# First batch's attention in 32x64 score tiles, turned in quarters, its values taken in halves, in two groups of blocks a pair

## The chip, the cores and the metric

The kernel runs on one core of a Trainium2 chip. The metric is device microseconds (us) of one execution, the median of several runs. Engines are called as the profile calls them: PE (TensorE matmul), PEld (its weight loads), DVE (VectorE), ACT (ScalarE), POOL (GpSimd), SP (the queue that issues most DMAs).

## The reference, cut to what matters

Windowed attention of 4 batches, 8 heads, 576 positions of 64, then two feed-forward layers over the 2304 tokens. Heads 0 to 3 see the last 32 positions, heads 4 to 7 see every fourth of the last 128.

```python
scores = scale * np.matmul(q, k.transpose(0, 1, 3, 2))
mask_plain = (rel >= 0) & (rel < window)                                   # window = 32
mask_dil = (rel >= 0) & (rel < window * dilation) & (rel % dilation == 0)  # dilation = 4
scores = scores - np.max(scores, axis=-1, keepdims=True)
attn = np.exp(scores); attn = attn / (np.sum(attn, axis=-1, keepdims=True) + 1e-09)
attn_out = np.matmul(attn, v)
x = g1(x @ w_in) @ w_out       # g1(h) = h - tanh(h)
x = g2(x @ w_in2) @ w_out2     # g2(h) = h / (1 + exp(-h))
```

The weights arrive in 64 bits and are turned on the chip into two f32 parts each ("high" and "low" words, then a leading and a trailing part).

## The kernel before, in words

The work on one batch's attention goes by pairs of heads, 4 pairs a batch: pairs 0 and 1 are plain, pairs 2 and 3 dilated (their positions are sorted by residue, so that a window of 32 neighbours remains). A pair's 576 queries are 9 blocks of 64 (`NB`, `QB`). In every tile the two heads of a pair stand above each other: rows 0 to 63 and rows 64 to 127.

For the first batch each pair goes through 3 units of 3 blocks (`UB`, `NU`). Of one unit: a matmul writes the mask into a PSUM bank (L401), six matmuls add 64x96 scores to it (64 queries of one head, 96 keys, L416), DVE takes the maxima (L451), ACT the exponentials, one instruction a block, with the sum on the side (L469), DVE the inverse sums (L474, L475), DVE or POOL scales (L479, `normed`), PE transposes three blocks of 96 keys (L501), ACT copies them to `pT` (L146), PE multiplies by the values (L510), ACT and DVE split the result into two parts of `X` (`x_hi`, `x_lo`, L553). Ahead of it PE transposes q and k (L363, L372), which ACT and DVE copy to qT and kT. An f32 matmul stands twice in the trace, since it is done in two passes, and an f32 transpose once.

From the second batch on a pair is done in two groups of 5 and 4 blocks (`GROUPS`), with 32x64 score tiles (L408): 32 queries of one head against 64 keys, four tiles of a block in four strips of 32 columns of the array. DVE transposes there what PE transposes in the first batch.

All this is mixed with the first feed-forward layer of block 0 (512 tokens, 16 slices `f` of the hidden width): per slice 12 matmuls into `h` and 12 into `y` (L578; four groups of three each), the gate (ACT L1146, DVE L1147), its two parts `gg` (ACT L146, DVE or POOL L1149), and the preparation of a piece of each weight matrix: three ACT operations (L180, L185, L146), DVE L190, POOL L194, and DVE or POOL L203.

The order of all engines up to the end of block 0's slices is set by a list of operations (`op(...)`) with the engines that may do each and a planned length, its predecessors and a rank; `play` walks through the list and gives each engine the operation that could begin first, by these planned lengths. Where it finds PE without work it puts in small matmuls on the identity (`idle`, L108). The engines then execute their streams in that order, each waiting for what it needs. SP's and POOL's DMA issues are in the list too. What follows block 0's slices is in a fixed order.

## Time and profile before

| | |
|---|---|
| median of 3 runs | 842.42 us (841.42 to 842.45) |
| the profiled execution | 843.15 us, of which 841.4 us from the first to the last instruction (the span) |
| PE busy | 828.4 us, 98% of the span |
| DVE, ACT, POOL busy | 68%, 50%, 24% |
| mean granted TensorE clock | 0.999 |

A row of the timeline gives the start, the length, engine, line, operation, what is written and read, and how many instructions are merged in the row; in brackets the idle time of the engine before it and what ended it. The distance between the starts of two neighbouring rows of a busy engine is what the first of them costs.

### The profile page before, as it was taken

The page shows a single profiled execution, that of the slowest core. Times are in us where ns is not written, and L with a number is a line of the kernel's source. Part 1 is how long each engine was busy: PE and PEld are TensorE (multiplying, and loading weights), DVE is VectorE, ACT ScalarE, POOL GpSimd, SP SyncE. Part 2 cuts the span into 40 slices and gives each one's busy share as a digit, 9 for nine tenths or more (in the row PEclk, how much of TensorE's full clock was granted, in tenths as well). Part 3 has the DMA queues.
Part 4 walks back from the last instruction along what each step waited for, and adds up shares of the span by engine and source line. Part 5 has one row for each costly group of instructions (what it writes and reads, how often), then busy time and mean ns, then how long its engine had stood idle before and what let it go on. Part 6 is the DMA issues. An engine that isn't in the chain of part 4 may idle for free.

```text
span 841.4 us, 16392 instructions
## 1 busy us (share of the span) xinstructions
PE 828.4 (98%) x6102; PEld 735.1 (87%) x6102; DVE 568.5 (68%) x1010; ACT 424.2 (50%) x960; POOL 198.9 (24%) x236
## 2 busy tenths in 40 slices
PE   8989999999999999999999999999999999999998
PEld 5767788888887888888899999888999999999997
DVE  3788987566676664566664677548766897567764
ACT  5898985355555443665553343445332454233442
POOL 8555442043333231111100000000025100054000
PEclk9999999999999999999999999999999999999999
DMA  9987353655569414477769199749897676998542
GB/s 219 296 219 196 83 141 91 179 124 120 125 142 260 101 43 147 152 268 267 281 240 374 50 366 360 265 150 365 298 409 265 245 287 253 341 353 290 184 169 57
DMA packets 168319, 184.58 MB, mean 219 GB/s; under 512 B 88848, under 2 KB 130864, under 8 KB 167216
## 3 DMA queue, kind: packets, MB, share of 16 engines
q1 hardware_dynamic: 167408, 182.69, 67.2%
q8 instruction: 48, 0.79, 0.4%
q0 software_dynamic: 832, 0.85, 0.4%
q14 instruction: 31, 0.25, 0.1%
HBM read 137.89 MB, written 45.61 MB: 218 GB/s over the span
## 4 chain that ended last, share of the span: by engine, by line
PE 92%; ACT 3%; DVE 2%; SPq 1%; issue 1%; DMA 0%; POOL 0%; ACTq 0%; DVEq 0%; POOLq 0%
PE y L578 43%; PE h L578 27%; PE q L578 16%; PE h L510 1%; SPq L301 1%; PE y L416 1%; PE s L408 1%; PE s L510 1%; PE y L974 1%; PE h L363 1%; PE y L501 1%; DVE pT L492 1%; PE o L510 1%; ACT st L180 1%; ACT st L185 0%
## 5 line engine op out<-in xcount | busy, mean ns | idle before, releaser
L578 PE MATMUL y<-gg,w 128*128 128x512 f32 (+1 forms) x960 | 218.3, 370 | 2.6 <-DVE gg L1149 2.6
L578 PE MATMUL h<-x,w 128*128 128x512 f32 (+1 forms) x960 | 218.4, 370 | 0.7 <-POOL w L203 0.7
L578 PEld LDWEIGHTS y<-gg,w 128*128 128x128 f32 x960 | 167.2, 189 | 34.4 <-DVE gg L1149 3.8
L578 PEld LDWEIGHTS h<-x,w 128*128 128x128 f32 x960 | 167.3, 189 | 31.8 <-POOL w L203 1.1
L578 PE MATMUL y<-wr,gs 128*128 128x256 f32 (+1 forms) x840 | 123.5, 298 | 0.0
L578 PEld LDWEIGHTS y<-wr,gs 128*128 128x128 f32 x840 | 112.6, 191 | 4.6
L726 ACT ACTIVATE G<-tmp 128x384 f32<-128x384 f32 (+1 forms) x48 | 32.9, 686 | 117.1 <-DVE tmp L717 117.1
L749 DVE TENSOR_TENSOR gs<-G,gs 128x768 fp32r<-128x768 f32 x64 | 62.7, 985 | 42.3 <-ACT gs L748 42.1
L748 ACT ACTIVATE gs<-G 128x768 fp32r<-128x768 f32 x64 | 53.5, 844 | 70.0 <-PE y L578 44.4
L578 PE MATMUL q<-x,wr 128*128 128x384 f32 x432 | 82.8, 335 | 0.0
L605 DVE TENSOR_TENSOR g<-h,g 128x512 f32<-128x512 f32 (+1 forms) x64 | 39.8, 622 | 59.3 <-ACT g L604 59.1
L578 PEld LDWEIGHTS q<-x,wr 128*128 128x128 f32 x432 | 75.5, 188 | 0.5 <-DVE tmp L717 0.5
L1463 ACT ACTIVATE gg<-g 128x512 fp32r<-128x512 f32 (+1 forms) x64 | 37.1, 579 | 74.7 <-DVE g L605 73.6
L604 ACT ACTIVATE g<-h 128x512 f32<-128x512 f32 (+1 forms) x64 | 34.7, 542 | 67.7 <-PE h L578 65.2
L1465 DVE TENSOR_TENSOR gg<-g,gg 128x512 fp32r<-128x512 f32 (+1 forms) x64 | 40.3, 630 | 41.7 <-ACT gg L1463 39.6
L727 DVE SCALAR_TENSOR_TENSOR G<-G,tmp 128x384 f32<-128x384 f32 (+1 forms) x48 | 41.3, 861 | 34.3 <-ACT G L726 34.3
L194 POOL TENSOR_TENSOR st<-st 128x512 int32<-128x512 int32 x36 | 39.6, 1109 | 78.3 <-DVE st L190 43.2
L578 PE MATMUL y<-x,wr 128*128 128x384 f32 x288 | 57.7, 334 | 0.0
L578 PE MATMUL h<-x,wr 128*128 128x384 f32 x288 | 57.7, 334 | 0.0
L578 PE MATMUL q<-wr,gs 128*128 128x256 f32 (+1 forms) x348 | 57.6, 301 | 0.0
L578 PEld LDWEIGHTS q<-wr,gs 128*128 128x128 f32 x348 | 49.3, 191 | 2.4
L578 PEld LDWEIGHTS y<-x,wr 128*128 128x128 f32 x288 | 50.6, 188 | 0.2 <-DVE x L638 0.2
(161 smaller groups left out, 1142.3 us busy)
## 6 DMA issues: line engine op xcount, KB each, us to landing
wr<-w_in SPq DMA_DIRECT2D x72, 512.0 KB
wr<-w_out SPq DMA_DIRECT2D x66, 512.0 KB
st<-in_moe_w_in_dram SPq DMA_DIRECT2D x32, 256.0 KB
st<-in_moe_w_out_dram SPq DMA_DIRECT2D x16, 512.0 KB
st_in<-in_moe_w_in_dram SPq DMA_DIRECT2D x32, 256.0 KB
w_in<-mixed SPq DMA_DIRECT2D x8, 1024.0 KB
wr<-w_in SPq DMA_DIRECT2D x24, 256.0 KB
x<-y_hi SPq DMA_DIRECT2D x6, 768.0 KB
```

The costliest lines, as they stand in the source:

```text
L180: engine.activation(out=high, in_=high, func=AF.Prelu, scale=2.0 ** -112, alpha=2.0 ** 32)
L194: engine.tensor_tensor(out=high, in0=high, in1=self.low.bitcast(I32), op=ALU.add)
L510: nc.tensor.matmul(o[64 * j:64 * j + 64, n - n0, :], self.v[j][:, n, :], pT[:, n, j, :], start=True, stop=True)
L578: nc.tensor.matmul(o, stat[a], mov[b], start=first and n == 0, stop=last and n == 2, skip_group_check=more)
L604: nc.scalar.activation(out=g, in_=h, func=AF.Tanh)
L605: nc.vector.tensor_tensor(out=g, in0=h, in1=g, op=ALU.subtract)
L726: nc.scalar.activation(out=g, in_=h, func=AF.Tanh, scale=0.5)
L727: return lambda: nc.vector.scalar_tensor_tensor(out=g, in0=g, scalar=1.0, in1=h, op0=ALU.add, op1=ALU.mult)
L748: nc.scalar.activation(out=gs[:, 0], in_=g, func=AF.Copy)
L749: nc.vector.tensor_tensor(out=gs[:, 1], in0=g, in1=gs[:, 0].bitcast(F32), op=ALU.subtract)
L1463: nc.scalar.activation(out=gg[:, 0], in_=g, func=AF.Copy)
L1465: nc.vector.tensor_tensor(out=gg[:, 1], in0=g, in1=gg[:, 0].bitcast(F32), op=ALU.subtract)
```

## The change

For the first batch alone:

- Two groups of blocks a pair (5 and 4) in place of three units of 3. The mask `mask` (96 keys wide) is gone; `near` (64 wide), which the later batches use, is built directly, by POOL on 32 rows and by three DVE copies, in place of an ACT copy and four later copies.
- Scores in 32x64 tiles, added to a mask of 64 columns.
- The four of the eight groups that `WHOLE` names take a shift on DVE (`shifted`), one ACT instruction for all exponentials of the group (`exps_whole`) and the sums on DVE (`totals`); the other four do one ACT instruction a block as before, over 64 columns.
- The probabilities are turned by ordinary matmuls against a reordered identity (`turn`), 128 rows by 32 columns each, four side by side in quarters of the array, and land as `turned`: 32 queries of both heads, 128 keys. ACT or DVE copies them.
- The values are taken in 64x64 quarters of the array, 32 columns each (`halves`), into two fixed banks, one for each half of a block's queries.
- v needs 32 more rows, a second copy of keys: one more load a head for pairs 0 and 1 (SP), a copy of 32 rows for pairs 2 and 3 (`double_v`). The values of pair 2 are loaded by SP, behind the first two weight pieces, in place of POOL.
- `pT` is zeroed later. Ranks and planned lengths of the list change.

```diff
     NM = NB + GROUPS[0][1]
-    mask = cpool.tile([P, NM, KB], BF16, name="mask")
-    nc.gpsimd.memset(mask[0:QB], 0.0)
...
-    nc.scalar.copy(out=mask[QB:], in_=half)
+    near = cpool.tile([P, NM, NARROW], BF16, name="near")
+
+    def build_near():
+        band = near[0:32, NM - 1]
+        nc.gpsimd.memset(band, 0.0)
+        keep(band, [[-1, NARROW]], 32, 1)
+        keep(band, [[1, NARROW]], -1, -1)
+        nc.vector.tensor_copy(out=near[0:32, :NM - 1], in_=band.unsqueeze(1).to_broadcast([32, NM - 1, NARROW]))
+        nc.vector.tensor_copy(out=near[32:QB], in_=band.unsqueeze(1).to_broadcast([32, NM, NARROW]))
+        for n in range(NB + 1):
+            for i in range(2):
+                for start in range(0, S, CLS) if n < NB else (0,):
+                    at = start - (QB * (n % NB) + 32 * i - 32)
+                    if 0 < at < NARROW:
+                        keep(near[0:32 * (i + 1), n, 0:at], [[0, at]], at - 33 + 32 * i, -1)
+        nc.vector.tensor_copy(out=near[QB:], in_=near[0:QB])
...
+                if self.first:
+                    out.append(lambda e, j=j, src=src: e.dma_start(
+                        out=self.v[j][KB:], in_=bass.AP(src.tensor, src.offset, [[D, P - KB], [QB * D, NB], [1, D]])))
             return out
+
+        def double_v(self, engine):
+            copy(engine, self.vt[KB:], self.vt[32:64])
...
             for n in range(n0, n1):
...
-                for j in range(2):
-                    nc.tensor.matmul(
-                        s[QB * j:QB * (j + 1), m, at:],
-                        self.qT[64 * j:64 * j + 64, QB * n:QB * n + QB],
-                        keys[64 * j:64 * j + 64],
-                        start=False, stop=n == n1 - 1,
-                    )
+                for i in range(2):
+                    q0 = QB * n + 32 * i
+
+                    at = HALO if masked and q0 == 0 else 0
+                    keys = self.kT[:, q0 - HALO + at:q0 + 32] if masked else kT1[:, q0:q0 + NARROW]
+                    for j in range(2):
+                        r = slice(64 * j, 64 * j + 64)
+                        nc.tensor.matmul(s[QB * j + 32 * i:QB * j + 32 * i + 32, n - n0, at:], self.qT[r, q0:q0 + 32], keys[r],
+                                         start=not masked, stop=not masked or n == n1 - 1)
...
+        def shifted(self, n0, n1):
+            nb = self.nb.pop(n0)
+            nc.vector.tensor_tensor(out=self.p[:, n0:n1], in0=self.ps.pop(n0), in1=nb.unsqueeze(2).to_broadcast([P, n1 - n0, NARROW]), op=ALU.add)
+
+        def exps_whole(self, n0, n1):
+            pr = self.p[:, n0:n1]
+            nc.scalar.activation(out=pr, in_=pr, func=AF.Exp)
+
+        def totals(self, n0, n1):
+            nc.vector.tensor_reduce(out=self.total[:, n0:n1], in_=self.p[:, n0:n1], axis=AX.X, op=ALU.add)
...
-            for m in range(UB):
-                nc.tensor.transpose(t[:, m, :], self.p[:, UB * u + m, :], one[F32])
...
+        def turn(self, n0, n1, bank):
+            t = bank[:, :(n1 - n0) * QB].rearrange("p (n j q) -> p n j q", j=2, q=32)
+            unit = one[F32].rearrange("p (j i q) -> p i j q", j=2, i=2)
+            self.pt[n0] = t
+            for n in range(n0, n1):
+                for g in range(4):
+                    i, kk = divmod(g, 2)
+                    kk ^= i
+                    nc.tensor.matmul(t[32 * g:32 * g + 32, n - n0], self.p[:, n, 32 * kk:32 * kk + 32], unit[:, i], start=True, stop=True)
...
+        def halves(self, n0, n1, at):
...
+            for n in range(n0, n1):
+                for i in range(2):
+                    r = slice(64 * i, 64 * i + 64)
+                    for j in range(2):
+                        nc.tensor.matmul(o[i][64 * j:64 * j + 64, n - n0], self.v[j][r, n], pt[r, n, j], start=True, stop=True)
...
-    SLOT0, SLOT, UNIT0, UNIT = 46.0, 5.2, 12.0, 1.8
+    SLOT0, SLOT, UNIT0, UNIT = 36.0, 5.2, 12.0, 4.5
...
-    NEXT0, NEXT = 60.0, 16.0
+    NEXT0, NEXT = 50.0, 16.0
+    WHOLE = (1, 0, 1, 0, 1, 0, 1, 0)
...
-            v_on = {"P": 0.62} if p.dil else {"S": 0.55}
...
+            on_p = p.c == NPAIR - 1
+            got[p, "v"] = [op({"P": 0.95} if on_p else {"S": 0.5}, fn, rank=p.c + (1.15 if p.dil else 0.2),
+                              late=0.25 if p.dil else 0.5, lag=3.0 if on_p else 0.0) for fn in p.v_loads()]
+            if p.dil:
+                got[p, "v"].append(op({"P": 1.5, "V": 0.8, "A": 1.1}, p.double_v, got[p, "v"], UNIT0 + UNIT * p.c, port=True))
```

Three places of the order. First PE, from the k transposes of pair 1 (`kin`) on. `one` and `late` are identities, `prob` the probabilities, `s` and `o` the banks of the values, `y_...` the banks of the scores and of the transposes. Before:

```order
L372 MATMUL h<-late,kin 64x96 x6
L401 LDWEIGHTS one
L401 MATMUL y_338<-mask,one 128x288
L416 MATMUL y_338<-kT,qT 64x96 x6
L501 MATMUL y_354<-late,prob 96x128 x3
L401 LDWEIGHTS one
L401 MATMUL y_359<-mask,one 128x288
L416 MATMUL y_359<-kT,qT 64x64 x2
L416 MATMUL y_359<-kT,qT 64x96 x4
L510 MATMUL o<-pT,v 64x64 x6
```

Of the change, after ten filler matmuls on `one` behind those k transposes:

```order
L410 MATMUL y_385<-near,one 128x320
L419 MATMUL y_385<-kT,qT 32x32 x2
L419 MATMUL y_385<-kT,qT 32x64 x18
L515 MATMUL y_415<-late,prob 32x64 x20
L515 MATMUL y_438<-late,prob 32x64 x16
L528 MATMUL s<-turned,v 64x32 x2
L528 MATMUL o<-turned,v 64x32 x2
```

Scores of pair 1 now come ahead of both turns and all values of pair 0, and one step holds 20 or 16 small matmuls where it held 6 or 3.

Second ACT, from the last scaled pieces of the attention to the first gate (`g<-h`): `st_...` are weight pieces, `w` their leading parts. Before, from the last turned copy on:

```order
L146 ACTIVATE pT<-y_804 96x384
L146 ACTIVATE w<-st_190 128x512
L185 ACTIVATE st_192<-st_192 128x512
L146 ACTIVATE x<-s 128x192
L180 ACTIVATE st_191<-st_191 128x512
L185 ACTIVATE st_191<-st_191 128x512
L180 ACTIVATE st_194<-st_194 128x512
L146 ACTIVATE w<-st_192 128x512
L185 ACTIVATE st_194<-st_194 128x512
L1146 ACTIVATE g<-h 128x512
```

Of the change, from the last turned copy that ACT does:

```order
L146 ACTIVATE turned<-y_954 128x320
L185 ACTIVATE st_198<-st_198 128x512
L180 ACTIVATE st_201<-st_201 128x512
L146 ACTIVATE w<-st_199 128x512
L146 ACTIVATE x<-s 128x5x32
L146 ACTIVATE x<-o 128x5x32
L146 ACTIVATE x<-s 128x4x32
L146 ACTIVATE x<-o 128x4x32
L146 ACTIVATE w<-st_198 128x512
L185 ACTIVATE st_201<-st_201 128x512
L180 ACTIVATE st_200<-st_200 128x512
L1190 ACTIVATE g<-h 128x512
```

When the attention's last `x` is written, ACT has issued 8 operations on weight pieces before the change and 12 with it.

Third PE again, where the second batch's first scores (32x64 tiles into `s` and `o`) stand among the feed-forward matmuls. Before:

```order
L578 MATMUL h<-x,w 128x512 x12
L408 MATMUL s<-kT,qT 32x64 x20
L408 MATMUL o<-kT,qT 32x64 x16
L578 MATMUL h<-x,w 128x512 x3
L578 MATMUL y_918<-gg,w 128x512 x3
```

Of the change:

```order
L607 MATMUL y_1118<-gg,w 128x512 x3
L607 MATMUL h<-x,w 128x512 x3
L607 MATMUL y_1119<-gg,w 128x512 x3
L607 MATMUL h<-x,w 128x512 x3
L607 MATMUL y_1120<-gg,w 128x512 x3
L419 MATMUL s<-kT,qT 32x64 x20
L419 MATMUL o<-kT,qT 32x64 x16
L607 MATMUL y_1121<-gg,w 128x512 x3
```

These scores stood behind 7 groups of three feed-forward matmuls and now stand behind 23; those of the next pair behind 17 and now behind 49.

## Rows read from the trace of the kernel before

**Rows 1.** The page: span, and PE's line (busy us, share, instructions).

```profile
span 841.4 us, 16392 instructions
PE 828.4 (98%) x6102; PEld 735.1 (87%) x6102; DVE 568.5 (68%) x1010; ACT 424.2 (50%) x960; POOL 198.9 (24%) x236
```

**Rows 2.** Busy time in four stretches (start:end, length, then each engine's us).

```profile
core 0: us, PE busy (x) PEld busy (x) DVE busy (x) ACT busy (x) POOL busy (x), PEclk, DMA share, GB/s
6.60:43.70 37.10, 34.85 (x580) 26.21 (x578) 22.99 (x71) 30.26 (x111) 24.27 (x50) 1.00 1.03 268
43.70:96.30 52.60, 48.14 (x435) 37.71 (x434) 44.62 (x85) 48.11 (x119) 28.45 (x27) 1.00 0.66 171
96.30:200.00 103.70, 103.70 (x775) 85.01 (x774) 73.17 (x141) 63.59 (x167) 32.01 (x40) 1.00 0.49 126
200.00:841.00 641.00, 636.65 (x4306) 584.35 (x4304) 427.14 (x714) 280.98 (x566) 108.16 (x107) 1.00 0.69 236
```

**Rows 3.** Timeline of PE: one unit's steps and a pair's k transposes.

```profile
28.05 0.30 PE L401 MATMUL y<-mask,one 128*128 128x288 bf16 x1
28.27 0.71 PE L416 MATMUL y<-kT,qT 64*64 64x96 f32 x12
28.92 0.57 PE L510 MATMUL o<-pT,v 96*64 96x64 f32 x12
29.42 0.53 PE L501 MATMUL y<-late,prob 128*96 128x128 f32 x3
29.88 1.22 PE L363 MATMUL h<-late,kin 72*64 72x72 f32 x32
```

**Rows 4.** Timeline of PE: the second batch's first scores.

```profile
47.63 0.76 PE L408 MATMUL s<-kT,qT 64*32 64x64 f32 x40
48.21 0.63 PE L408 MATMUL o<-kT,qT 64*32 64x64 f32 x32
48.77 0.96 PE L578 MATMUL h<-x,w 128*128 128x512 f32 x3
```

**Rows 5.** Timeline of PE: the rows with idle time ahead, 6.6 to 100 us.

```profile
11.19 0.72 PE L372 MATMUL h<-late,qin 96*64 96x96 f32 x12 [1.04 <-ACT kT L146]
...
39.04 0.53 PE L501 MATMUL y<-late,prob 128*96 128x128 f32 x3 [1.09 <-POOL prob L479]
...
45.13 2.57 PE L578 MATMUL h<-x,w 128*128 128x512 f32 x10 [0.66 <-POOL w L203]
...
50.29 1.65 PE L578 MATMUL y<-gg,w 128*128 128x512 f32 x6 [0.56 <-DVE gg L1149]
...
58.13 0.76 PE L408 MATMUL s<-kT,qT 64*32 64x64 f32 x40 [1.24 <-DVE kT L393]
...
72.15 0.96 PE L578 MATMUL y<-gg,w 128*128 128x512 f32 x3 [1.70 <-DVE gg L1149]
...
95.98 0.98 PE L578 MATMUL y<-gg,w 128*128 128x512 f32 x3 [0.30 <-DVE gg L1149]
```

**Rows 6.** Timeline of ACT around the mask copy.

```profile
9.12 1.31 ACT L250 COPY mask<-mask 64x1344 bf16<-64x1344 bf16 x1
10.46 1.18 ACT L146 ACTIVATE kT<-h 128x288 f32<-128x288 f32 x2
```

**Rows 7.** Chain that ended last: six records of ACT's exponentials (three blocks).

```profile
36.81 0.96 ACT prob L469 x6
```

**Rows 8.** Groups by line and shape, 0 to 100 us (busy us, mean ns).

```profile
L146 ACT ACTIVATE pT<-y 96x384 f32<-96x384 f32 x12 | 5.8, 486 | 2.4 <-PE y L501 2.1
L451 DVE TENSOR_REDUCE sum<-prob 128x5 f32<-128x320 f32 x3 | 1.4, 476 | 0.0
```

**Rows 9.** Chain that ended last, ahead of the wait at 72.15.

```profile
67.08 2.21 DMA kin<-in_k_dram
69.41 0.13 DVE kT L393
...
71.40 0.70 DVE gg L1149
```

**Rows 10.** Timeline of PE: the attention's last values.

```profile
43.16 0.57 PE L510 MATMUL s<-pT,v 96*64 96x64 f32 x12
43.74 0.73 PE L578 MATMUL h<-x,w 128*128 128x512 f32 x2
```

More of the change, by code (lines that the diff above doesn't have):

```diff
@@ L255, in tile_kernel @@
     qT1 = cpool.tile([P, S], F32, name="qT")
-    near = cpool.tile([P, NM, NARROW], BF16, name="near")
     pT = cpool.tile([KB, NB, 2, QB], F32, name="pT")
-    nc.gpsimd.memset(pT, 0.0)
+    turned = [cpool.tile([P, NB, 2, 32], F32, name="turned")]
     class Pair:
@@ L514, in values @@
             if self.dil:
-                parts = [(a, b, src[:, a - s0:b - s0]) for a, b in self.cut(s0, s1)]
+                out = [(self.columns(a, b), src[:, a - s0:b - s0]) for a, b in self.cut(s0, s1)]
             else:
@@ new lines, in tile_kernel @@
+            ring_t.leave(b)
+            a = op({"T": 0.15 + 0.115 * m}, lambda e, p=p, g=g, i=i: p.halves(*g, 160 * (i % 3)), [b, *got[p, "v"], *ring_o.take()], r)
+            if n1 == NB:
+                ring_v.leave(a)
+            ends = []
+            for z in range(2):
+                b = op({"A": 0.32}, lambda e, p=p, n0=n0, z=z: p.x_hi(e, (n0, z)), [a], r)
+                ends.append(op({"V": 0.32}, lambda e, p=p, n0=n0, z=z: p.x_lo((n0, z)), [b], r))
+            ring_o.leave(*ends)
@@ L1038, in tile_kernel @@
+            x_done.setdefault(p.c, []).extend(ends)
+            if n1 == NB:
                 at_v = 4 * p.c + 2
@@ L1076, in tile_kernel @@
                 in_room[NF - len(MORE_IN) + place - 1 - len(MORE_OUT)] = (c,)
-        left = {"bank": tuple(x_done[NPAIR - 1][-2:]), "pT": tuple(ring_v.take() + ring_v.take() + ring_v.take()),
+        left = {"bank": tuple(x_done[NPAIR - 1]), "pT": (),
                 "q": (), "k": (), "v": (first[2].last,)}
         normed = {}
-        def narrow(e, g):
-            copy(e, near[32 * g:32 * g + 32], mask[32 * g:32 * g + 32, :, 32 * (g % 2):32 * (g % 2) + NARROW])
-        narrows = [op({"V": 0.35, "P": 0.9}, lambda e, g=g: narrow(e, g), x_done[0][:1], NEXT0 - 30, port=True) for g in range(4)]
+        zero = op({"P": 1.05}, lambda e: e.memset(pT, 0.0), x_done[0][:1], NEXT0 - 10)
+        left["pT"] = (zero,)
         def front(p):
```

140 lines of the change are left out of this document (64 added, 76 removed).

## Prediction

> **What bounds the kernel now.** I read the page first: PE is busy in 828.4 of 841.4 us [rows 1]. A share over the whole span hides where PE waits, so next come four stretches [rows 2]. From 96.3 to 200 us PE is busy in all of the 103.7 us, and after that in 636.65 of 641. What the change can win there is only what arrives from ahead of it: the order behind is fixed and its loads are set off by PE's own progress, so I take it that each us won before 96 is a us won at the end. Ahead of it lie two stretches of different kinds. Up to 43.7 us, the attention of the first batch, PE is busy 34.85 of 37.1 us and ACT 30.26. From 43.7 to 96.3, block 0's feed-forward, PE is busy 48.14 of 52.6 us, but ACT also 48.11 and DVE 44.62: there the feeding of PE is nearly as full as PE. The timeline of PE then gives the waits [rows 5]: seven, 6.59 us in all, two in the attention (1.04 and 1.09) and five behind it (0.66, 0.56, 1.24, 1.70, 0.30; 4.46 together). So two things count: PE's work up to the last values, which end at 43.74 [rows 10], and the waits behind.
>
> **Scores.** A unit cost PE 0.87 us, from the mask at 28.05 to the values at 28.92 [rows 3]; twelve are 10.4. The new tiles are those of the second batch: 20 matmuls in 0.58 us (48.21 - 47.63), 16 in 0.56 with the switch to other work behind them [rows 4]. The mask took 0.22 for 288 columns [rows 3]; 0.24 and 0.21 for 320 and 256. With 0.1 for the switch behind the first group a pair costs 1.14 + 0.45 + 0.1 = 1.7, four pairs 6.8: **3.6 us less**.
>
> **Turning.** A transposed unit cost 0.46 (29.88 - 29.42), twelve 5.5 [rows 3]. The new matmuls stream 64 columns through 32, as the scores in rows 4 do, but over 128 rows, and no row shows four quarters of that height. Rows 4 show four quarters in step (40 records of 216 ns and more fit into 0.58 us only side by side), and the k transposes show two halves of 72 rows in step (32 records in about 1.1 us) [rows 3]. If four run in step, a pair costs 1.24 and all 5.0; if only two, by the pace of the values (0.50 for 12 records, about 0.058 for two), some 9.6. I take 5.0, since the strips of rows 4 are as narrow: **0.5 less** (bounds 0.5 less to 4.1 more).
>
> **Values.** 0.50 a unit, twelve 6.0 [rows 3]. Now 36 matmuls a pair, 72 records, stream 32 columns into four quarters. With four in step at half the 0.056 of rows 4 a pair costs 0.8, all 3.2; two in step at 0.058 as before, 1.35 and 5.4. I take 4.0: **2.0 less** (0.6 to 2.8). The Trainium skill, page TensorEngine Tiling (Array Packing), section Instruction Overhead, speaks against this part: a matmul carries about 60 cycles of overhead, one with a free size of 1 lasts as long as one of 60, and a tiling factor should not be taken from a small dimension. By it the 32 columns would cost nearly what 64 do, an estimate of 5.4 for all values and 1.4 us off the gain. The trace shows no tile of 32 columns; it shows only that a record of rows 4 costs 14 ns, which leaves room.
>
> **Start.** The mask copy held ACT from 9.12 to 10.43, and pair 0's kT copies, 0.59 each, waited for it [rows 6]; PE waited 1.04 us for them [rows 5]. Now they run from 9.12, the second (PE delivers at 9.9) to 10.57, and the first scores begin at 10.85, not 11.90: **1.05 less**. POOL's nine selects and a last DVE copy of about 0.4 us make the new mask at 9.7 by my count, behind a memset that waits for the warm-up's tile, so this rests on ACT.
>
> **New waits in the attention.** I walked the new order step by step with these lengths and, for DVE on 320 columns, 0.4 us (476 ns a record, a little overlapped [rows 8]). Pair 0's turn stands behind pair 1's k copies on DVE and pair 1's scores on PE. Pairs 2 and 3 wait near 31 us for sums and scaling, since ACT does a copy of 32x1152 (1.1 us by the mask copy's 1.31 for 1344 [rows 6]) and two weight operations ahead of their exponentials. From 10.85 to the last values PE has 6.9 us of q and k transposes, 6.8, 5.0 and 4.0 from above, three feed-forward groups of 0.68, and by the walk 2.1 us of waits and filler: it ends at 37.7. Before, the same stretch held 1.09 of waits. So the last values come at 37.7, not 43.7: **6.0 us less** (3.6 + 0.5 + 2.0 + 1.05, less 1.1 of new waits).
>
> **Behind the attention.** ACT's share of the first batch falls: 36 exponentials of 0.32 [rows 7] are 11.5 us; now 4 of 0.45 and 16 of 0.32 make 6.9. Of 12 turned copies (0.39 apart, 4.7 in all [rows 8]) two stay on ACT, 0.9. The mask copy's 1.3 goes, the v copy's 1.1 comes, the x copies grow from 5.0 to 5.8. Sum 22.5 to 14.7, **7.8 less on ACT**; the order shows the use, 12 weight operations issued at the attention's end against 8. DVE gets shifts, sums and six turned copies and loses shorter maxima and four mask copies; its work up to the last x is about as before, 23 us. So the weights are there not only 6 us earlier but some 2 us earlier against the feed-forward. Of the five waits, 1.24 is PE waiting for DVE's kT of the second batch, and 1.70 is `gg` waiting on DVE behind the same transposes, which wait for a DMA of kin [rows 5, 9]. In the new order the scores that need these stand 16 and 32 groups (0.68 us each) later, while SP, which has 15 more loads ahead of them, is later by about 3 to 9 us by the bytes and the issues. I let both waits go, 2.94 us, keep the other three (1.5) as they are, in part as a wait for the first gate, and add 0.9 for what ACT and DVE, still nearly full, will hold up: **2.0 less**.
>
> **Sum.** 6.0 + 2.0 = 8.0 us. The span goes from 841.4 to 833.4, the profiled execution from 843.15 to 835.15. That execution is 0.7 above the median of the runs, 842.42, so the median becomes **834.4**.
>
> **The rivals.** A is this forecast (chance 0.53): 831 to 838.
>
> B, the attention's chain is bound by DVE and ACT, not PE (0.17). DVE was busy 22.99 of 37.1 us [rows 2] and needs the same in 27; each group passes it three to five times, and ACT's wait for pair 2's v, loaded late by SP, lies on the same chain. Then PE's saved work turns into waiting; only the start and the later waits are won, 3.0 us: 839.4. For it speaks how full DVE gets, against it that two groups and two pairs are in flight. The Trainium skill has it as a rule, same page, section PSUM Bottleneck: TensorE gets faster by tiling, the copies out of PSUM do not, and after a fourfold gain they may bound. Whether it bears here no row of before can show.
>
> C, no wait takes the place of any (0.12): 6.1 + 1.05 + 1.09 + 4.46 = 12.7: 829.7.
>
> D, block 0 is bound by ACT, with its 48.11 of 52.6 us, and PE gives the lead back in waits for weights and `gg` (0.10): 842.4. Against it stand ACT's 7.8 us.
>
> E, the turning quarters do not run in step (0.08). Then 72 records a pair take 0.056 each, 4.2 us with the switches, 17 in all in place of 5.0: 12 us onto the forecast, 846.4. It decides from 13.0 us on, 0.15 for four records side by side. Against it: the halves of 72 rows in rows 3.
>
> **How the numbers follow.** A measurement of this kernel can tell about 0.2%, 1.7 us, from no change. A, B and C lie beyond it: faster 0.82. D is no change, 0.10. E is slower, 0.08. The range reaches from C's end to B's, 829.5 to 840.5, and leaves out D, E and a little of C. A's own range, 831 to 838, holds the bounds of values, new waits and of the 0.9.
>
> **What would show it.** Scores: 0.95 and 0.8 us a group on PE, mask included. Turning: 36 matmuls in about 1.25 us a pair; 2.4 would be two in step, 4 E. Values: 1.0 a pair; 1.35 is the rule on overhead. The first scores at 10.9, the last values near 37.7; if PE waits there for DVE's sums or turned copies, it is B. Then the rows of PE with idle time ahead: those on kT and on `gg` at 72 us should be gone. Waits on L203's weights of more than 4 us together would be D. The forecast is wrong if the last values come after 41 us, if waits behind them exceed 5 us, or if PE loses its full share after block 0.

## The result, and the profile after

The changed kernel takes **851.43 us** (median of 4 runs, 848.63 to 854.16) against 842.43 for the kernel before on the same chip: a ratio of 1.0106, 95% interval 1.0065 to 1.0148. It is slower by 9 us, and the forecast of 834.4 with its range to 840.5 was wrong in sign and size. The profiled execution took 853.24 us.

The page of the changed kernel, its span and its rows of PE and of the granted clock (40 slices):

```profile
span 851.5 us, 17442 instructions
PE 834.7 (98%) x6647; PEld 742.0 (87%) x6647; DVE 567.4 (67%) x1007; ACT 415.5 (49%) x919; POOL 193.8 (23%) x228
PEclk9589999999999999999999999999999999999999
```

Beside [rows 1] the share of PE is the same 98% and PE has 545 more matmuls (and as many more weight loads). New is the last line: slices 2 and 3 of the clock's row are not at 9, where the kernel before has 9 throughout. PE's timeline says whether the pieces cost what was forecast (start, length, instruction, idle time ahead in brackets):

```profile
10.69 0.30 PE L410 MATMUL y<-near,one 128*128 128x320 bf16 x1
10.92 0.76 PE L419 MATMUL y<-kT,qT 64*32 64x32 f32 x40
11.61 0.23 PE L108 MATMUL y<-one 128*128 128x128 bf16 x1
11.68 0.27 PE L410 MATMUL y<-near,one 128*128 128x256 bf16 x1
11.88 0.65 PE L419 MATMUL y<-kT,qT 64*32 64x64 f32 x32
12.46 0.23 PE L108 MATMUL y<-one 128*128 128x128 bf16 x1
16.50 1.21 PE L515 MATMUL y<-late,prob 128*32 128x64 f32 x72
23.19 0.31 PE L528 MATMUL s<-turned,v 64*64 64x32 f32 x1 [4.61 <-issue]
41.23 0.40 PE L372 MATMUL h<-late,qin 72*64 72x72 f32 x2 [2.50 <-issue]
55.04 0.24 PE L528 MATMUL o<-turned,v 64*64 64x32 f32 x1 [0.59 <-issue]
131.56 1.23 PE L607 MATMUL h<-x,w 128*128 128x512 f32 x3 [0.29 <-ACT w L146]
137.65 1.66 PE L607 MATMUL y<-gg,w 128*128 128x512 f32 x6 [1.44 <-DVE gg L1193]
```

Scores and turning do: a first score group takes 0.92 us (10.69 to 11.61), a second 0.78, a pair is turned in 1.21, and the first scores begin at 10.69. (The values do not; they come below.) But from 18.6 on stand three waits whose releaser is "issue": by the legend PE waited for nothing that the profile shows. The last two rows are the longest of the waits that are left behind the attention. Windows cut at these places and at the changes of the clock (start:end, length, busy us and instructions of PE, PEld, DVE, ACT, POOL; then the granted clock, the DMA engines' share, GB/s):

```profile
6.56:18.58 12.02, 11.76 (x338) 9.06 (x336) 6.62 (x18) 6.17 (x17) 9.05 (x22) 1.00 1.10 221
18.58:20.21 1.63, 0.00 (x1) 0.00 (x0) 0.52 (x3) 0.00 (x0) 0.89 (x2) 1.00 1.10 259
20.21:23.19 2.98, 0.00 (x0) 0.00 (x1) 0.00 (x0) 0.00 (x0) 0.83 (x1) 0.50 0.96 260
23.19:37.28 14.09, 14.09 (x336) 12.28 (x336) 6.39 (x18) 7.05 (x21) 1.67 (x3) 0.50 0.57 160
37.28:40.69 3.41, 1.45 (x47) 1.08 (x48) 1.25 (x4) 3.34 (x13) 3.35 (x3) 1.00 1.04 392
40.69:41.22 0.53, 0.00 (x0) 0.00 (x0) 0.00 (x0) 0.53 (x4) 0.07 (x1) 0.50 0.99 361
41.22:47.52 6.30, 6.29 (x103) 4.86 (x106) 2.99 (x10) 1.23 (x3) 2.55 (x3) 0.50 1.07 378
47.52:55.70 8.18, 7.42 (x315) 6.02 (x303) 4.68 (x16) 5.45 (x19) 4.26 (x7) 1.00 0.66 120
55.70:96.30 40.60, 40.38 (x337) 32.04 (x338) 34.25 (x68) 39.90 (x98) 21.05 (x21) 1.00 0.68 184
96.30:200.00 103.70, 101.97 (x831) 82.63 (x830) 75.73 (x147) 63.21 (x164) 36.14 (x44) 1.00 0.51 129
200.00:841.00 641.00, 640.30 (x4299) 586.42 (x4298) 430.60 (x719) 287.07 (x589) 111.86 (x109) 1.00 0.69 236
```

PE stands for 4.61 us, and DVE and ACT run dry with it; only the DMA engines are busy throughout. Behind the stop lie 14.09 us in which PE is busy all the time at a granted clock of 0.50, the lower of its two levels (1.2 of 2.4 GHz), and 6.30 more behind the second stop. So the last values end at 55.7 us and not at 43.7 [rows 10]. The waits behind them are 1.95 us against 4.46 [rows 5].

What PE waits for shows in the DMA view. First the stretch from the middle of pair 0's work to 20.6 us, then the next 1.3 us (queue, kind: packets, MB, share of 16 engines):

```profile
q1 hardware_dynamic: 1009, 0.96, 90.5%
```

```profile
q1 hardware_dynamic: 379, 0.30, 91.2%
q8 instruction: 1, 0.02, 5.7%
```

Queue q8 moves packets of 16,384 bytes marked "instruction", 53 in the whole run; PE's trace has 13,526 recorded instructions (13,294 of them weight loads and matmuls), and 13,526 / 53 is about 256 a packet. I counted PE's recorded instructions in order of start. The three waits stand after number 705, 1473 and 2241, each 768 = 3 x 256 behind the last. I call such a count a border. A table from the trace, with the packets taken in order (us); "one border earlier" is the start of the first instruction past the border 256 before, "border reached" the start of the last instruction ahead of this one:

```
kernel   border  one border   packet  landed  border   next
                 earlier      starts          reached  instruction
before     705     20.71      22.15   23.32   27.20    27.26
before    1217     33.54      37.36   38.47   45.13    45.23
after      705     16.04      20.67   21.85   18.36    23.19   stop
after      961     23.19      24.30   25.61   28.12    28.12
after     1473     34.13      38.98   39.96   38.51    41.23   stop
after     2241     51.28      52.76   53.78   54.23    55.04   stop
```

Read so, PE asks for a page of 256 instructions when it passes the border one page ahead. In the table the packet starts 1.1 to 4.9 us after that crossing (the runs below show that this hangs on what the DMA engines have queued) and takes about 1.1 us, and where PE had to stop it goes on some 1.3 us after the landing. Before, 256 instructions lasted 6.3 us and more in the attention, so the packet always came in time. The changed kernel runs through 256 in 2.3 us (16.04 to 18.36): four small quarters of four instructions each (two passes of weight load and matmul) stand where one transpose of two was. That is theory T1, the instruction supply. The Trainium skill, page Runtime: NRT & Kernel Launch, section Instruction fetch mechanics, has the page size (16 KiB blocks, 256 instructions, one fetched while the last is executed), which these packets agree with; it calls the cost mostly hidden, which holds for the kernel before and not here, and its size of PE's store (128 KiB) doesn't fit a stop one page behind a late packet.

### The profile page after: what moved, and what is told of

The parts are those of the page before. It is cut to its first block, busy times and chain, and to the rows that moved or that the text cites. A ratio compares the mean times of both kernels' runs of the same rounds, so it can differ in the third digit from the quotient of the medians.

```text
span 851.5 us, 17442 instructions
## 1 busy us (share of the span) xinstructions
PE 834.7 (98%) x6647; PEld 742.0 (87%) x6647; DVE 567.4 (67%) x1007; ACT 415.5 (49%) x919; POOL 193.8 (23%) x228
## 4 chain that ended last, share of the span: by engine, by line
PE 86%; DVE 5%; ACT 3%; DMA 2%; issue 2%; SPq 1%; POOL 0%; DVEq 0%; POOLq 0%; ACTq 0%
PE y L607 40%; PE h L607 24%; PE q L607 15%; DVE pT L502 1%; PE h L372 1%; ACT prob L468 1%; PE y L419 1%; DMA st<-in_moe_w_out_dram 1%; DMA w_out<-o_mixed 1%; PE s L528 1%; PE s L419 1%; PE h L543 1%; PE y L1004 1%; SPq L304 1%; PE y L515 1%
```

## The experiments

Rivals to T1 were T2 (the stopped matmul waits for data that the trace doesn't name), T3 (small tiles bring the clock down by themselves, and the rest follows) and T4 (sheer traffic, not queued loads, delays the packets). Each ratio is to the kernel before, run beside it on the same chip, with its 95% interval. Line numbers in rows are those of each run's own kernel. In every run the stops are counted by PE's recorded instructions as above, and a stop is the time from the last instruction's start ahead of a border to the next one's; so taken the changed kernel's three are 8.4 us, of which PE is idle for 7.7.

**e1, the same program with 64 more PE instructions in the warm-up.**

```
-    WARM = 12
+    WARM = 8
+        for n in range(36):
+            nc.tensor.matmul(bank[0:32, 0:64], warm[:, 0:32], warm[:, 0:64], start=True, stop=True)
```

> The changed kernel with 64 more instructions on PE ahead of everything else: in the warm-up 4 of the 12 wide matmuls give way to 36 small ones (32x32 weights, 64 columns). The program behind the warm-up is the same. Theory T1 (PE runs out of instructions: in the changed kernel it stands still exactly after its recorded instructions 705, 1473 and 2241, 768 apart, and goes on 1.3 us after a 16 KB packet of the queue marked instruction has landed): the stops come after instructions 705 and 1473 again, so 64 instructions earlier in the program, the first one at the beginning of the values of pair 0's second group and no longer near their end, the second among the scores ahead of the q transposes. T2 (the stopped matmul waits for data, v or the turned probabilities, which the trace does not name): the stop stays at the same matmul, the last third of these values, whatever its number. The time says little, 848 to 853 us by both.

The stop came after 705 again, so 64 instructions earlier in the program: PE's timeline of e1 has it at the fourth matmul record of the values.

```profile
17.69 0.30 PE L528 MATMUL s<-turned,v 64*64 64x32 f32 x3
21.49 0.24 PE L528 MATMUL s<-turned,v 64*64 64x32 f32 x1 [3.51 <-issue]
```

T2 is out. The second stop was not where I had put it: the packet for 1473 was in time here (landed 34.26, border 36.26), and the other stops came at 1729 and 1985, borders too. 851.51 us in one run.

**e2, two wide matmuls where four quarters turned** (pairs 0 and 1 in both halves, 2 and 3 in one; v's rows 64 to 127 loaded in plain order).

```
-                for g in range(4):
-                    i, kk = divmod(g, 2)
-                    kk ^= i
-                    nc.tensor.matmul(t[32 * g:32 * g + 32, n - n0], self.p[:, n, 32 * kk:32 * kk + 32], unit[:, i], start=True, stop=True)
+                for i in range(2):
...
+                        nc.tensor.matmul(t[64 * i:64 * i + 64, n - n0], self.p[:, n], unit[:, i], start=True, stop=True)
```

> The changed kernel with fewer instructions for the same turning: one matmul of 64 columns in place of two quarters of 32, in pairs 0 and 1 for both halves (v's lower rows then hold keys in plain order), in pairs 2 and 3 for one of the two. 216 PE instructions fewer of some 1,900 in the attention. T1: the first stop moves on in the program by the 72 instructions saved in pair 0, to the transposes behind the values, and shortens from 4.8 us to some 4; the second moves on by 144 and more, and the last values come 3 to 6 us earlier than at 56 us; time 844 to 849 us against 851.4. T2: the stop stays in the values of pair 0 and the time within 2 us of 851.4. By its work alone turning would cost 0.3 us more a pair in pairs 0 and 1, since only two matmuls lie side by side.

851.9 us, 1.008 (1.0055 to 1.0106). The stops fell from 8.4 us together to 5.2 (3.3 after 705, 1.5 after 1473, 0.4 after 1729), all at borders, and the half clock from 23.9 us to 13.7, but the last values still ended at 55.2 us, and the time did not move beyond its spread (846.4 to 853.6). PE's rows of pair 2's turning show what took the gain back:

```profile
41.53 0.33 PE L518 MATMUL y<-late,prob 128*64 128x64 f32 x2
41.79 0.30 PE L516 MATMUL y<-late,prob 128*32 128x64 f32 x4
42.02 0.33 PE L518 MATMUL y<-late,prob 128*64 128x64 f32 x2
```

One wide tile and two quarters in turn cost 0.49 us a block (41.53 to 42.02) and 4.45 a pair (to 45.98), at full clock, where four quarters cost 1.21 a pair. The two dilated pairs so got 6.5 us of new work on PE; I had not counted it. So e2 does not show what fewer stops are worth, and e4, e7, e8 and e10 carry the same work (0.77 us a block at half clock in e7 and e10).

**e3, SP's loads behind pair 1's held until pair 0 is scaled; e4, the same with e2's edit.**

```
+        hold = op({"V": 0.1}, lambda e: e.tensor_copy(out=first[2].room("qin")[0:32, 0, 0, 0:1], in_=first[0].p[0:32, 0, 0:1]), ...)
+        for p in first[2:]:
+            for o in (got[p, 0], got[p, 1], *got[p, "v"][:-1]):
+                o.after.append(hold)
...
+            a = op({"S": 1.1 if ch.is_in else 0.55}, lambda e, ch=ch, st=stage[1]: ch.load(st), [*stage[3], hold], ...)
```

> The changed kernel with the same PE program but for the order that the planner makes around later loads: SP's loads behind pair 1's (q and k of pairs 2 and 3, v of pair 2, all weights, the second batch's q and k) are held by a copy of one scaled probability of pair 0 into pair 2's q tile, and POOL issues pair 3's v behind the scaling, so that the DMA engines are nearly empty when PE crosses instruction 449 at 16 us. T1: the instruction packet that started 4.6 us after this crossing starts within 2.5 us of it, the stop after 705 falls from 4.8 us to under 2.5, and the clock stays full or falls for a far shorter time; the time depends on what the held weights cost later, 843 to 853. T2 (data): the stop stays as long as it was. T3 (the small tiles bring the clock down by themselves, and the stops follow from it): the clock falls to half at the same work, near 20 us, whatever the stop does.

> Both edits, fewer turning instructions and held loads. T1: the first stop is under 1.5 us or gone, and the time lies below both single edits, 838 to 848 us. T2 and T3: no better than the better of the two alone.

e3 took 857.84 us, 1.0163 (1.0147 to 1.0179), e4 860.23, 1.0187 (1.0148 to 1.0226). The table's columns for both:

```
e3         705     15.63      16.37   17.49   17.93    19.17   stop
e3        1217     24.70      29.32   30.42   30.04    31.86   stop
e4         705     16.53      17.23   18.15   19.33    19.45
e4        1217     24.80      29.02   30.12   27.94    31.55   stop
```

With the queues empty the packet started 0.7 us after its crossing, not 4.6; the first stop fell to 1.2 us and in e4 it was gone. That is T1's forecast for the packet and the stop. The held loads then came in one rush, and the next packets waited 4.2 to 4.6 us: the stop moved on. In e4 the clock was full until 30.75 us, through 20 us of the same 32-row score tiles and 32-column values, and fell 2.6 us after its stop began: T3, as stated, is out (e9 below, with the quarters too, kept its full clock to 40.5). My times for both were too low; I had not counted the rush, nor e2's work in e4.

**e5, the start term by itself, in the kernel before.**

```
-    nc.scalar.copy(out=mask[QB:], in_=half)
+    nc.vector.tensor_copy(out=mask[QB:], in_=half)
```

> The kernel before with one line changed: the copy of the mask's second half goes from ACT to DVE. It tests the start term by itself, without a single new PE instruction. If the term is right (PE waits 1.04 us at 11.19 only because ACT does this copy from 9.12 to 10.43), the first values come some 1 us earlier and the time falls by 1.05 us, to about 0.9987 of before. The rival: DVE, which copies q at that time, is late in its turn and the wait only changes its name: ratio 1.000.

843.9 us, 1.0005 (0.9989 to 1.002): nothing won. Timelines of PE and POOL in e5:

```profile
10.37 0.29 PE L401 MATMUL y<-mask,one 128*128 128x288 bf16 x1
27.44 1.25 POOL L335 DMA_DIRECT2D v<-in_v_dram  x2 [0.45 <-DMA v<-in_v_dram]
28.71 1.30 POOL L479 TENSOR_TENSOR prob<-prob,sum 128x288 f32<-128x288 f32 x2
29.44 0.53 PE L501 MATMUL y<-late,prob 128*96 128x128 f32 x3 [1.48 <-POOL prob L479]
```

and POOL in the kernel before:

```profile
28.03 0.64 POOL L335 DMA_DIRECT2D v<-in_v_dram  x1 [0.71 <-DMA v<-in_v_dram]
28.68 0.68 POOL L479 TENSOR_TENSOR prob<-prob,sum 128x288 f32<-128x288 f32 x1
```

The first scores do begin 1.5 us earlier (the mask's matmul at 10.37). At 28.7, as before to 0.03 us, POOL scales probabilities behind its loads of v, which wait for earlier loads to land, and PE gives 1.48 us back there; the last values end at 43.80. The attention of the kernel before runs into the loads. The ratio is the rival's, but not its reason: the wait at 11.19 did go.

**e6 to e8, paced loads**: behind each big load of SP one small load into a spare tile (e8: two). SP's loads take turns on eight semaphores, so fewer big ones are under way. e7 and e8 have e2's edit too.

```
+    def paced(out, in_):
+        nc.sync.dma_start(out=out, in_=in_)
+        nc.sync.dma_start(out=spare[:, c:c + 2], in_=q[0, 0, 0:1, 0:2])
```

> The changed kernel with the same PE program, and behind each of SP's big loads (q and k of pairs 2 and 3, the first block's weights) a load of 8 bytes into a spare tile. SP's loads take turns on eight semaphores, so that at most eight are under way; the small ones halve what is under way of the big ones. T1 (PE's instruction packets queue behind loads already issued): the packets start 1 to 3 us after the crossing that asks for them, where 4.6 and 4.9 were seen, the stops at 705, 1473 and 2241 fall from 8.4 us together to under 5, the time with them, 842 to 850. Rival T4 (what delays a packet is not how much is issued ahead but the sheer traffic, or what comes from POOL's queue): the packets start as late as before, the time stays at 851 or rises by what SP's extra issues of 0.4 us each cost the loads.

> The same with the fewer turning instructions of the second run. T1: with shorter packets' waits and 216 instructions fewer the stops fall under 2.5 us together and the clock stays full for longer: 836 to 846, the first version that could come out under the kernel before. T4: as the second run, 852.

> Two 8-byte loads behind each big one, so that fewer than three big ones are under way. T1: packets start within 2 us of their crossing, no stop over 1 us, and either the clock stays full and the time is 835 to 843, or the loads themselves come too late (an issue of 0.4 us for each small one, and the DMA engines partly idle) and PE waits for q, k or weights instead, by name: 843 to 855.

e6: 848.19 us, 1.004 (1.002 to 1.006), 5.6 us better than the changed kernel by the ratios, and inside the range given for it. The packets started 0.8 to 2.5 us after their crossings; the stops fell from 8.4 to 4.0 us, the last values to 48.4. So what is queued ahead matters, and T4, as stated, is out. e7: 857.98, 1.0157 (1.0129 to 1.0185); e8: 861.1, 1.0201 (1.0175 to 1.0227). Their stops were 1.95 and 1.3 us only, but they carry e2's work, and their loads came late, e8's by choice and e7's at one place, here with ACT's row and PE's behind it:

```profile
36.58 1.16 ACT L146 ACTIVATE v<-v 32x1152 f32<-32x1152 f32 x1 [6.93 <-DMA st<-in_moe_w_in_dram]
39.18 0.43 PE L430 MATMUL y<-kT,qT 64*32 64x64 f32 x4 [5.79 <-DVE kT L148]
```

The copy that doubles pair 2's v stands in ACT's order ahead of pair 2's exponentials and waits for loads. (The trace names a weight load as the releaser; v's own loads, which share SP's semaphores with it, are what the copy reads.) Behind this wait the clock stayed at half from 35.22 to 65.94 us.

**e9 and e10, e6 and e7 with pair 2's v loaded right behind its q and k** (and longer planned lengths for SP's loads in the list).

```
-                rank=p.c + (1.15 if p.dil else 0.2)
+                rank=p.c + (0.15 if p.dil else 0.2)
```

> The paced version of the sixth run (8-byte loads behind the big ones), with v of pair 2 loaded right behind q and k of pair 2 and no longer behind those of pair 3 and two weights, and the planner told what SP's loads cost now. In the seventh run ACT stood 6.9 us in a copy of v's rows for pair 2, whose loads were late, and PE 5.8 us behind it. T1 with that second cause: stops of PE after instructions 705, 1473, 1985 and the like of 4 us together as in the sixth run, no wait for v's copy, last values 2 to 4 us earlier than the 48.4 us there; 840 to 847 us. If late loads are the greater part by now, the stops hardly matter and the last values come before 44 us: under 842.

> The same with the fewer turning instructions. T1: the stops fall to 2 us together, as in the seventh run (1.95), and without its wait of 5.8 us behind v's copy the clock has no reason to stay at half from 35 to 66 us: last values before 46 us, 838 to 846 us. If the clock falls near 22 to 25 us as in the sixth and seventh runs, some 5 us of that are lost to it. A rival for the clock (it falls with the small tiles alone): half clock at the same place whatever stops and waits are left.

e9: 847.73 us, 1.006 (1.0037 to 1.0084); e10: 855.59, 1.0158 (1.0109 to 1.0207). e9's windows up to 44 us, then e10's from 36 to 60:

```profile
6.60:20.00 13.40, 12.09 (x370) 9.51 (x371) 7.16 (x20) 6.18 (x17) 9.79 (x24) 1.00 0.88 182
20.00:40.50 20.50, 16.06 (x627) 13.34 (x624) 12.83 (x38) 12.09 (x44) 8.04 (x9) 1.00 0.66 199
40.50:44.00 3.50, 3.50 (x76) 2.64 (x75) 2.78 (x7) 3.35 (x8) 0.22 (x2) 0.51 0.80 258
```

```profile
36.00:60.00 24.00, 23.86 (x297) 16.74 (x296) 8.42 (x25) 9.15 (x28) 4.63 (x7) 0.50 0.88 256
```

e9 ran its attention at full clock up to 40.5 us although it stopped at five borders, 6.3 us in all, and ended the last values at 45.5; its time lies just above the range given for it. e10 had stops of 2.4 us only, yet PE worked at half clock for 30.7 us from 31.79, busy in 23.86 of 24. I had written that the clock had no reason to stay down there: wrong.

**e11, turning by transposes of two blocks at once**, 10 PE instructions a pair and not 144; v is laid out in two halves of rows by even and odd blocks, and loaded in more pieces. **e12, the same with e9's loads.**

```
+                nc.tensor.transpose(bank[:, k * P:(k + 1) * P], self.padded[:, 2 * m:2 * m + 2].rearrange("p n k -> p (n k)"), one[F32])
...
+                            nc.tensor.matmul(o[b][64 * j:64 * j + 64, k, i], self.v[j][r, m, i], pt[r, m, j, i], start=True, stop=True)
```

> The changed kernel with the turning done by transposes again, one of 128x128 for two blocks of 64 keys (groups of 4 and 5 blocks, two blocks' probabilities side by side in the columns, one block's 64 keys in each half of the rows; v is laid out to fit, 16 loads a dilated pair and no copy). A transpose is two instructions where a quarter was four, so a pair turns with 10 PE instructions and not 144, 536 fewer in all, and the scores, the values and their 32-column tiles are as in the changed kernel. Loads are issued as they were. T1: the last values lie some 500 instructions earlier, so two of the page borders in the attention are gone; the stop at 705 falls on work one to two us later and shrinks from 4.8 us to 2 to 4, all stops together from 8.4 to 3 to 6. Turning itself costs 0.6 us a pair in place of 1.2 (0.115 each by rows 3). Time 838 to 848 us. A rival: v's 16 loads on SP and POOL for each dilated pair come too late, and PE waits for v by name: 848 or more.

> The same with the paced loads (small loads, now of 4 bytes, behind the big ones) and v of pair 2 early, as in the ninth run. T1: there the stops were 6.3 us together, 0.85 to 1.95 each, each by instruction packets that came 3.6 us and more after their crossing; with 24% fewer instructions in the same stretch PE needs a page 1 us later, so most of them fall under 0.4 us, together under 2. The last values come by 41 us (45.5 in the ninth run, less 4 of stops, less 2.4 of turning, plus new waits), and the time is 833 to 841 us, the first under the kernel before. If it stays over 842 with stops under 2 us, instruction supply is not what holds the attention any more, and the waits by name say what does.

e11: 847.27 us, 1.0033 (1.002 to 1.0045), with its other loads as in the changed kernel: some 6 us won by the ratios, of which about 2 are the turning itself: at full clock it takes 4.9 us in quarters and 2.7 in this form (e16's rows). One stop is left, the first, and behind it the half clock (PE's row, then the window):

```profile
22.54 0.24 PE L555 MATMUL s<-turned,v 64*64 64x32 f32 x1 [2.76 <-issue]
```

```profile
22.50:40.50 18.00, 17.96 (x313) 14.67 (x317) 9.76 (x28) 10.14 (x29) 3.09 (x5) 0.53 0.61 161
```

e12: 852.73, 1.0096 (1.0076 to 1.0115), with 0.9 us of stops but many small waits for data by name (pair 3's q, scaled probabilities, turned copies), 6.3 us idle up to the last values and 10.2 us of half clock ahead of them. It was above the 842 that I had set as the mark for "supply is no longer what holds it".

**e13 to e15, e11 with pair 3's loads of v behind pair 0's scaling on POOL**; e14 has the first weights behind pair 2's v as well, e15 e6's paced loads.

```
+        hold = op({"P": 0.2}, lambda e: e.tensor_copy(out=first[NPAIR - 1].vt[64:96, 0, 0, 0, 0:1], in_=first[0].p[64:96, 0, 0:1]), ...)
```

> The eleventh run's kernel (turning by transposes of two blocks) with one change: POOL's 16 loads of v of pair 3, issued from 7 to 19 us there and not needed before 30, wait for pair 0's first scaled probabilities (a copy of one of them into v's tile ahead of the loads), near 15 us. They carry about 1 MB, some 4.5 us of the 213 GB/s moved there, out of the way of the packet that PE asks for at 16.4. T1: that packet starts 1 to 2 us after its crossing, not 3.3, the stop at 705 falls from 2.8 to under 1 us, and if the clock keeps full then, the last values come near 40 us and not 49.4: 834 to 841 us. Rival: waits for data (q and k of pair 3, v of pair 2, weights) that the half clock hid show by name and add up to 5 us and more, or the clock falls all the same: 843 to 849.

> The same, and the first two chunks of weights (1 MB) behind v of pair 2 on SP's queue, no longer ahead. It takes these out of the way of the second and third packets and brings pair 2's v some 3 us earlier, the first weights some 7 us later, to about 30 us, where the first feed-forward groups want them. T1: stops under 1 us, last values by 40 us if the clock keeps full, 833 to 841. Rival: the feed-forward groups that fill the attention's gaps come too late, PE waits for weights by name: 842 to 848.

> As e13, with the small loads behind the big ones as in the sixth run. There the packets came 1.0 to 2.5 us after their crossings. T1: no stop over 0.5 us at all; q, k of pair 3 and v of pair 2 come some 2 us later by SP's extra issues, which PE may wait for once or twice. 834 to 844. Rival as for e13: 845 to 853.

e13: 850.74 us, 1.0076 (1.0052 to 1.0099); the packet still started 3.4 us late, the stop stayed at 3.0: a miss. The held loads carry 0.57 MB and not the 1 MB that I had counted, and what SP had queued was enough to keep the packet waiting. e15: 851.71, 1.0083 (1.0055 to 1.011): stops of 1.2 us, and waits for kT and probabilities in their place. e14: 847.69, 1.004 (1.0006 to 1.0074), and its ten times fall into two groups, 842.4 to 845.3 and 850.1 to 853.1. Its profile, from the lower group, has a stop of 0.9 us at 705 and one of 1.3 at 1473; of the upper group there is no trace, only a lower mean clock (0.985 to 0.990 against 0.991 to 0.996).

**e16, e14 with e1's 64 instructions in the warm-up; e17, the kernel before with them.**

> The fourteenth run's kernel with the 64 more instructions in the warm-up that the first run had. The program crosses instruction 449 then near 13.7 us and needs the packet at 18.0, 4.3 us later, where it was 15.4 and 18.6, 3.2 later; with a packet 1 to 2 us on its way to the start, 1.2 to 1.6 in its transfer and 1.3 to PE's next instruction, the stop at 705 goes or stays under 0.3 us. T1 with the clock following the stops: no half clock near 21 us, the group at 850 is gone, the median 838 to 844 us. Rival: the stop only moves to the next border (961, PE gets there sooner now), with the clock behind it, and the time is spread as before, 842 to 853.

> Control: the kernel before with the same 64 instructions more in its warm-up. It has 2.7 to 3.9 us to spare at its first borders (the packet landed at 23.32, the border was reached at 27.2), so that by T1 nothing changes: ratio 1.000 within 0.003, no stop at any border. If the 64 instructions by themselves cost or win something, it shows here.

e16: **843.3 us**, 0.9993 (0.9975 to 1.001). All twelve times lie between 842.4 and 845.0; the upper group is gone, the stop at 705 too (packet landed 17.07, border reached 19.59), and the clock is full up to 37.88 us. Instructions that do nothing took 4 us off the median of e14, and the stop at 705 with it. In the kernel before they cost rather than won: 1.002 (1.0002 to 1.0037), no stop. Most of what PE waits for in e16 now has names (three of PE's waits, then ACT's row):

```profile
PE y L534 <- ACT st L180: 1.8, 1, 1.8
PE s L555 <- DVE x L610: 1.5, 1, 1.5
PE o L555 <- issue: 0.9, 1, 0.9
```

```profile
33.80 0.66 ACT L180 ACTIVATE st<-st 128x512 f32<-128x512 f32 x1 [2.85 <-DMA st<-in_moe_w_in_dram]
```

**e18, e16 with the planner told that the first weights land 4.5 us later.**

> The sixteenth run's kernel with the planner told that the first four weight chunks land 4.5 us later than it thought, so that ACT does pair 2's exponentials, turned copies and x ahead of the first weight operation and no longer behind it. If the waits behind that operation (2.85 us of ACT, 1.46 and 1.77 of PE) are what holds the attention now, PE's idle time up to the last values falls from 5.7 to 3 to 4 us and the time by 1.5 to 2.5 us, 840 to 842.5, ratio 0.996 to 0.999. If the feed-forward groups only come that much later, the waits move behind the attention and the time stays at 843 to 845.

849.96 us, 1.0062 (1.004 to 1.0083): worse. PE's rows:

```profile
24.61 0.40 PE L392 MATMUL h<-late,kin 72*64 72x72 f32 x5 [1.81 <-issue]
41.18 0.90 PE L534 MATMUL y<-late,prob 128*128 128x128 f32 x3 [3.08 <-POOL prob L512]
```

A stop came back at border 961 (its packet started 3.0 us after the crossing), and the wait behind ACT's weights gave way to one of 3.08 for POOL's scaling. The theory that this one wait held the attention is not borne out, but the test isn't clean: with the stop came 10.2 us of half clock. No version beat the kernel before; e16 equals it.

## Why the prediction was wrong, step by step

**Scores, turning, start: right as prices.** 0.92 and 0.78 a group against 0.95 and 0.8; 1.21 a pair against 1.25, so the quarters do run in step and rival E is out; the first scores at 10.69 against 10.85. But the twelve transposed units of the kernel before cost 4.9 us in all, not 5.5 (the one unit that the forecast multiplied was a long one), so the turning won nothing.

**Values: mis-sized.** PE's row of five blocks' first values at full clock, and the next work behind them:

```profile
49.13 0.25 PE L528 MATMUL s<-turned,v 64*64 64x32 f32 x2 [0.17 <-DVE turned L148]
49.84 0.96 PE L607 MATMUL h<-x,w 128*128 128x512 f32 x3
```

They cost 0.71 us, and four blocks 0.60 (27.62 to 28.22 in e9, where no stop cuts them): 1.3 a pair, 5.3 for all, where the forecast took 4.0 and its mark was 1.0 a pair. Their 40 records start 14.5 ns apart (49.13 to 49.69), and so do those of 64 columns in [rows 4] (0.58 us for 40). So half the columns saved next to nothing a record, and the values won 0.6 us (5.9 to 5.3), not 2.0. The 1.35 a pair that the prediction set down for the overhead rule (the Trainium skill, page TensorEngine Tiling (Array Packing), section Instruction Overhead) is about what came out, and the trace agrees with that rule. The prediction's other way to this price, two quarters in step and not four, would come to the same, and no run tells the two apart.

**New waits in the attention: the step that failed.** The walk took PE's instructions as always there and its clock as full, and gave 2.1 us of waits, last values at 37.7. They came at 55.7, 18 us later. The stops account for 7.7 us (4.61 + 2.50 + 0.59). The windows hold 14.09 + 6.29 us of PE's work at clock 0.50. What that cost shows in pieces that stand at both levels, such as the scores of five blocks:

```profile
34.97 1.29 PE L419 MATMUL y<-kT,qT 64*32 64x32 f32 x40
36.19 0.32 PE L528 MATMUL s<-turned,v 64*64 64x32 f32 x2
```

They take 1.22 us at 0.50 and took 0.69 at full clock (10.92 to 11.61); five blocks' values take 1.22 (30.24 to 31.46) and 0.71. By that 20.4 us of work would have been some 12 at full clock, an estimate of 8 to 9 us lost. Together that is 16 to 17 of the 18 us, and the values' 1.3 are most of the rest. That the stops are those of the instruction supply is shown by e1 (they keep their number and change their place), e3 and e6 (they shrink with what is queued ahead of the packet) and e16 (with the place of the border); e11 agrees, with fewer instructions. That the half clock follows from the stops is shown only in so far as it falls behind them and not with the small tiles by themselves (e4, e9). I had counted the matmuls of each piece by time alone; the order of the change showed from the start that there are more of them, 545 by the page.

**The start's 1.05 us to the end: not in the kernel before**, by e5: 1.5 us won at 10.4 are lost at 28.7, where POOL's loads set the time. No run takes this term by itself out of the changed kernel. The premise "each us won before 96 is a us won at the end" is another matter: in the changed kernel what was lost there did arrive, as the sum below shows.

**And the walk had too few other waits.** In e16, without the stop at 705 and with 3.41 us of half clock, PE is idle for 5.9 us up to the last values (at 47.1), 1.2 of it at borders, where the walk had 2.1 with its fillers: nearer to rival B, the chain through ACT, DVE and the loads. What the change would have given without any stop no run shows; e16, whose turning is cheaper by 2 us and whose loads come in another order, gave about no change.

**Behind the attention: the sum was about right**, 1.95 us of waits against some 2.4 (1.5 + 0.9). I can't say that its reason was: PE came 12 us late to these stages, which would let any wait go.

**The sum.** 12.0 us later at the last values, 2.5 less behind, 0.5 more idle after 200 us: 10.0 of the 10.1 by which the span grew. "Wrong if the last values come after 41 us" was the mark that told it; none of the rivals had the mechanism.

## What to carry to other kernels

Count instructions on the tensor engine, not only time: here 256 of them had to last longer than the way of one 16 KB packet through the loaded queues, 3.5 to 7.2 us from crossing to next instruction in the stops tabled above. Cutting tiles into narrow ones bought some 4 us of engine time at full clock (scores from 10.2 to 6.8, values from 5.9 to 5.3, turning nothing) and multiplied the instructions just where loads were dense. A stop named "issue" at counts of 256 apart is the sign, and the remedies that shortened stops here are fewer instructions, fewer loads queued at that time, or another place for the border; none of them made a kernel faster than the one before the change, so look also for what waits behind the stops.

## What the hardware did that was not expected

- **The half clock outlasts its stop by far and costs as much again** (8 to 9 us against 7.7 in the changed kernel). After the stop at 18.6 us PE was busy in all of 14.09 us at 0.50; in e10 it was 23.86 of 24 us. So a busy PE is not enough to raise it. In after and e11 it fell 1.6 to 3.7 us after a stop began; e9 stopped for 1.04 and 0.63 us and kept its full clock, e14 for 0.71 and did not, and the kernel before waited 1.70 us [rows 5] without a fall. It fell behind waits for data too: at 73.05 us in e5, behind 2.11 us for `gg`. What decides between these is open; none of the runs isolates it.
- **A late instruction packet costs about 1.3 us beyond its landing** (21.85 to 23.19, 39.96 to 41.23, 53.78 to 55.04), and 1.3 to 1.7 in the stops of the other runs.
- **Tiles of unlike width in turn are dear**: 0.49 us a block in e2, against 0.13 (1.21 / 9) for four quarters.
- **Times in two groups 8 us apart may come from a border**: e14's 842 and 850 became e16's 843 with 64 idle instructions more, which by themselves won nothing in e17. No trace of the upper group shows it directly.
